# Wider weight conversion, three-instruction operand sums, and the order of the first norms in a fused attention and Fourier-mixing kernel

## The chip, the cores and the metric

The kernel runs on one core of a Trainium2 chip. A core has a matrix engine (TensorE, "PE" in the profile, with its weight loads "PEld"), a vector engine (VectorE, "DVE"), a scalar engine (ScalarE, "ACT"), GpSimd ("POOL") and SyncE ("SP", which here only issues DMAs). Each engine works through its own queue in order and waits for the others by semaphores. The metric is the device time in microseconds, as the median of several runs.

## The reference

Attention over 4 batches, 8 heads, 768 tokens and 64 columns per head, then a Fourier mixing block over the 512 columns of all heads, all in float32:

```python
k_sum = k.reshape(B, H, nb, 32, D).max(axis=3)      # 24 blocks of 32 keys
v_sum = v.reshape(B, H, nb, 32, D).mean(axis=3)
scores_l = where(|i - j| < 16, q @ k.T / sqrt(D), -1e9)
scores_s = q @ k_sum.T / sqrt(D) + log(32)
a = softmax(concat(scores_l, scores_s));  attn = a @ concat(v, v_sum)
x = attn as (B, S, 512)
u = x + real(fft(fft(x, axis=1), axis=2))
un = (u - mean(u)) / sqrt(var(u) + 1e-6)
out = u + relu(un @ w_ch1) @ w_ch2                  # 512 -> 2048 -> 512
```

The two weight matrices arrive as 64-bit floats and are handled as pairs of 32-bit words.

## The kernel before, in words

**Stages.** Batch 0's attention runs first and by itself (`first_attention`, L844), for 4 pairs of heads: `prepare` turns q and k with products against an identity (L714) and takes the maxima of key blocks (L696); `wide_scores` makes band scores (L744) and summary scores (L748) in two halves, their exponentials (L750) and a mask product; `sum_values` puts the value sums into `vw` (L763); `wide_values` makes the weighted values (L771), divides by the sums and writes them to `x`. The folds that prepare `x` for the transform follow (`fold_sequence`, `fold_halves`, `fold_ends`). In this function the order on TensorE and VectorE is the program's, by `manual_schedule`; elsewhere a scheduler orders instructions by priority and readiness, except where `issue_after(mark)` puts an instruction behind a marked one.

Then comes `gen_fourier` (L1198) for batch 0: a transform over tokens (products `y`, L1232 and L1236, copied out by ScalarE at L1237 and L1238), and one over columns (products `mx`, L1259 and L1261, six tiles of 128 tokens). Each tile is added to `x`, its statistics are taken (L1266, L1267), and per half of three tiles a chain of 14 small VectorE instructions (L1279 to L1291) makes the norm's scale and shift by an inverse square root. Then every tile is normalised into `un` (L1304 on ScalarE for odd tiles, L1307 on VectorE for even ones), transposed (`unt`, L1312) and copied into `u` (L1313).

The dense part follows: `gen_hidden` (L1319) and `gen_out` (L1375), with both products by a Strassen-Winograd scheme: an operand's four blocks are joined by four sums or differences, and seven block products replace eight. `_left_sums` and `_right_sums` (L477, L484) make these sums. Operands are tiles with seven slots, in the order

```python
A11, A12, S3, A22, S1, S2_, S4 = range(7)
B11, T3, B21, B22, T1, T2, T4 = range(7)
A21, B12 = S3, T3
```

Batches 1 to 3 are the same, with a narrower form of attention (`gen_attention`, L974: scores L787 and L804, values L822 and L827) woven between the dense products of the batch before. `drive(...)` (L1478) steps several generators in turn, in given proportions and priorities.

**Weights.** While batch 0 runs, `gen_weights` converts the 64-bit weights: `load_raw` (L1057) fetches pieces of 512 columns into `words`, four buffers deep; `convert` (L1071) masks exponent and mantissa on VectorE (L1081, L1082), rescales both on ScalarE (L1083, L1084), puts in sign and low word on VectorE (L1086, L1088) and multiplies. Two such pieces and the sums make one weight tile (`make`, L1094), and 16 weights are made: 8 of `w_ch1` and 8 of `w_ch2`, in the order of `plan` (L1051). The finished tile is also stored for the later batches.

**Small tables.** At the start ScalarE's queue issues DMAs for `ident`, `wide`, `count`, `sel` and `half_of`. The last has 128 x 2 numbers and serves `vs`, the value sums of batch 1 and later: a memset and L1507 fill it. Loads of q, k, v, tables and raw weights go through SP's queue, in program order (`fetch`, L551).

Of the kernel before, what the change touches and what calls it, by code (L numbers as in the profile page):

```python
# [10 lines left out]
I32 = mybir.dt.int32  # L11
U32 = mybir.dt.uint32
AF = mybir.ActivationFunctionType
# [463 lines left out]
def _left_sums(tt, a):  # L477
    tt(a(S1), a(A21), a(A22), ALU.add)
    tt(a(S3), a(A11), a(A21), ALU.subtract)
    tt(a(S2_), a(S1), a(A11), ALU.subtract)  # L480
    tt(a(S4), a(A12), a(S2_), ALU.subtract)


def _right_sums(tt, b):  # L484
    tt(b(T1), b(B12), b(B11), ALU.subtract)
    tt(b(T2), b(B22), b(T1), ALU.subtract)
    tt(b(T3), b(B22), b(B12), ALU.subtract)
    tt(b(T4), b(B21), b(T2), ALU.subtract)


def _main_program(ctx, tc, q, k, v, moe_w_ch1, moe_w_ch2, out):
# [72 lines left out]
    dense_bank = bank  # L564

# [278 lines left out]
    def first_attention():  # L844
# [8 lines left out]
        for g in range(NP - 1):  # L853
            p[g + 1] = wide_scores(0, g + 1, (lambda: add_blocks(1)) if g == 1 else None)
            wide_values(0, g, p[g], x)
            if g == NP - 2:
                block_sums(1, 0)
            load_values(*following(0, g, 2))
            for par in range(2):
                fold_sequence(par, g)  # L860
            if g < NP - 2:
                prepare(0, g + 2)
                sum_values(0, g + 1)
            if g == NP - 3:
                load(1, 0)
                get_tables(0, lambda: load_raw(1))
                load_raw(2)
                sum_values(0, g + 2)
        fold_halves(0, 0)
        wide_values(0, NP - 1, p[NP - 1], x)  # L870
        for par in range(2):
# [102 lines left out]
    def gen_attention(b):  # L974
# [13 lines left out]
        for g in range(NP + 1):  # L988
# [22 lines left out]
            if g < NP:  # L1011
                held = scores(b, g)
                if (b, g) == (1, 1):
                    key_maxima(g)
# [12 lines left out]
            if (b, g) == (1, 0):  # L1027
                for h in range(2):
                    with tc.issue_after(marks["norm"]):
# [41 lines left out]
    def convert(piece, dst):  # L1071


        n = 2 * HD
        i = pieces.index(piece)
        load_raw(i + 3)
        raw = raws[i]
        tmp = words[:, 4096 + 1024 * (i % 2):5120 + 1024 * (i % 2)].rearrange("p (a n) -> p a n", a=2)
        low, high = raw.bitcast(U32)[:, :, 0], raw[:, :, 1]
        ex, man = tmp[:, 0, :].bitcast(I32), tmp[:, 1, :].bitcast(I32)  # L1080
        nc.vector.tensor_scalar(out=ex, in0=high, scalar1=0x7FF00000, scalar2=None, op0=ALU.bitwise_and)  # L1081
        nc.vector.tensor_scalar(out=man, in0=high, scalar1=0x000FFFFF, scalar2=None, op0=ALU.bitwise_and)  # L1082
        nc.scalar.activation(out=ex, in_=ex, func=AF.Relu, bias=rebias, scale=8.0)  # L1083
        nc.scalar.activation(out=tmp[:, 1, :], in_=man, func=AF.Copy, bias=1.0, scale=2.0 ** -20)  # L1084
# [3 lines left out]
        nc.vector.scalar_tensor_tensor(out=tmp[:, 1, :], in0=low, scalar=2.0 ** -52, in1=tmp[:, 1, :],  # L1088
                                       op0=ALU.mult, op1=ALU.add)
        yield  # L1090
        tt(dst, tmp[:, 1, :], tmp[:, 0, :], ALU.mult)
        yield

    def make(f, j):  # L1094
# [8 lines left out]
        for hh in range(2):  # L1103
            yield from convert((f, j, hh), wv[:, 2 * hh:2 * hh + 2].rearrange("p a n -> p (a n)"))
        if f == 1:
            _left_sums(tt, lambda i: wv[:, i])
# [3 lines left out]
        else:  # L1110
            _right_sums(tt, lambda i: wv[:, i])
# [37 lines left out]
    def get_w2(b, j):  # L1149
# [4 lines left out]
        if b == 1 and j < NC:  # L1154
            marks["load"] = fetch(out=w[:, 0:4], in_=dw2[j][:, 0:4])
            _right_sums(lambda *a: to_sum.append((tt, a)), lambda i: w[:, i])
# [41 lines left out]
    def gen_fourier(b):  # L1198
# [44 lines left out]
        norms = []  # L1243
        for half in range(2):
# [5 lines left out]
            for i in range(HT):  # L1250
# [4 lines left out]
                else:  # L1255

                    ps = bank([P, 2, HD], f"mx_{b}_{t}")
                    for par in range(2):
                        nc.tensor.matmul(ps[:, par, :], yt[:, half, 2 * par, cols], fd[:, 3 * par, :],  # L1259
                                         start=True, stop=False)  # L1260
                        nc.tensor.matmul(ps[:, par, :], yt[:, half, 2 * par + 1, cols], fd[:, 3 * par + 1 + half, :],  # L1261
# [325 lines left out]
```

## Time and profile before

| | before |
|---|---|
| median of 3 runs | 803.74 us (803.03 to 804.97) |
| the profiled execution | 806.53 us, of which the span 804.7 us |
| PE busy | 779.7 us (97%) |
| PEld busy | 568.9 us (71%) |
| DVE busy | 496.4 us (62%) |
| ACT busy | 231.5 us (29%) |
| POOL busy | 47.3 us (6%) |
| mean granted TensorE clock | 0.986 |

The span goes from the first to the last instruction. The page divides it into 40 slices of 20.1 us and gives each engine's busy share in tenths. A row "PEclk" gives the clock that TensorE was granted, in tenths of full speed. The timeline lists instructions in order of time, merged where several alike follow each other; in brackets stands how long the engine sat idle before, and which event ended the wait. A line number can be that of a helper: L567 is the one through which most two-input VectorE operations go, and L553 the one that issues DMAs.

### The profile page before, as it was taken

Reading aid. Unit: us, or ns where it says so; the run is one execution under the profiler, and the core shown is the slowest. Engines: PE = TensorE matmul, PEld = TensorE weight load, DVE = VectorE, ACT = ScalarE, POOL = GpSimd, SP = SyncE. Lnnn points to the kernel's source line nnn. Section 1 sums busy time; section 2 is a strip of 40 time slices with the busy share of each in tenths; the row PEclk is TensorE's granted clock in tenths of the full one; section 3 lists DMA queues with packets and bytes.
Section 4 is the critical chain, followed back from the end, with each engine's and each line's share of the span. In section 5 each row is a group of like instructions: output and inputs, shape, how many; then the busy total and the mean of one; then the engine's idle time right before and its main releaser. Section 6 shows DMA issues by size and latency. Waiting matters only on the chain.

```text
span 804.7 us, 14470 instructions
## 1 busy us (share of the span) xinstructions
PE 779.7 (97%) x5914; PEld 568.9 (71%) x5914; DVE 496.4 (62%) x1119; ACT 231.5 (29%) x523; POOL 47.3 (6%) x85
## 2 busy tenths in 40 slices
PE   7978899999999999999999999999999999999996
PEld 5767755445579866688569866688669875786685
DVE  3789799696988737663577635563576623533441
ACT  3542756535636112200126112210126102001200
POOL 0000000000000011200120010300130000000000
PEclk8999799999999999999999999999999999999999
DMA  9798398698665358995354159620513153105001
GB/s 225 144 263 189 120 273 256 230 240 279 167 204 161 79 171 185 259 148 131 123 189 138 54 190 194 175 86 1 229 56 138 53 196 140 57 0 230 0 27 55
DMA packets 133355, 121.84 MB, mean 151 GB/s; under 512 B 94464, under 2 KB 114912, under 8 KB 133088
## 3 DMA queue, kind: packets, MB, share of 16 engines
q1 hardware_dynamic: 132016, 118.53, 53.2%
q0 software_dynamic: 576, 2.10, 0.7%
q8 instruction: 48, 0.79, 0.4%
q10 hardware_dynamic: 688, 0.20, 0.1%
q14 instruction: 27, 0.22, 0.1%
HBM read 97.22 MB, written 23.59 MB: 150 GB/s over the span
## 4 chain that ended last, share of the span: by engine, by line
PE 86%; DVE 9%; ACT 2%; DMA 1%; issue 1%; ACTq 0%; DVEq 0%
PE hx L1338 19%; PE ox L1407 18%; PE hz L1338 9%; PE oz L1407 9%; PE hy L1338 5%; PE o L1384 5%; PE oy L1407 5%; PE y L1232 3%; PE mx L1191 2%; PE sc L787 2%; PE av L822 2%; PE unt L1312 2%; DVE w L567 1%; PE av L827 1%; DMA half<-c_half 1%; DVE x L567 1%
## 5 line engine op out<-in xcount | busy, mean ns | idle before, releaser
L1338 PE MATMUL hx<-u,w 128*128 128x384 f32 x512 | 185.1, 490 | 1.7 <-ACT h L1349 1.1
L1338 PEld LDWEIGHTS hx<-u,w 128*128 128x128 f32 x512 | 95.3, 190 | 70.4 <-ACT p L793 4.4
L1338 PE MATMUL hz<-u,w 128*128 128x384 f32 x256 | 93.5, 486 | 0.0
L1407 PE MATMUL oz<-w,s 128*128 128x256 f32 x336 | 81.5, 380 | 0.0
L1407 PE MATMUL ox<-w,s 128*128 128x256 f32 x336 | 80.3, 380 | 0.0
L1407 PE MATMUL ox<-w,h 128*128 128x256 f32 x336 | 79.9, 381 | 0.0
L567 DVE TENSOR_TENSOR x<-ox,x 128x256 f32<-128x256 f32 x84 | 35.3, 423 | 67.5 <-PE ox L1407 67.3
L1338 PEld LDWEIGHTS hz<-u,w 128*128 128x128 f32 x256 | 48.5, 190 | 34.3 <-ACT h L1357 0.9
L1407 PEld LDWEIGHTS ox<-w,h 128*128 128x128 f32 x336 | 63.0, 190 | 11.1 <-issue 1.2
L1407 PEld LDWEIGHTS ox<-w,s 128*128 128x128 f32 x336 | 63.0, 190 | 9.4 <-DVE x L567 0.8
L1407 PEld LDWEIGHTS oz<-w,s 128*128 128x128 f32 x336 | 63.4, 190 | 8.6
L1349 ACT COPY h<-hx 128x384 f32<-128x384 f32 x32 | 15.3, 477 | 185.0 <-PE hx L1338 185.0
L567 DVE TENSOR_TENSOR h<-hy,h 128x384 f32<-128x384 f32 x32 | 17.8, 557 | 48.8 <-PE hy L1338 48.6
L1338 PE MATMUL hy<-u,w 128*128 128x384 f32 x128 | 46.6, 487 | 0.6 <-DVE h L567 0.6
L567 DVE TENSOR_TENSOR h<-hx,h 128x384 f32<-128x384 f32 x32 | 17.8, 556 | 43.9 <-PE hx L1338 43.2
L1384 PE MATMUL o<-w,h 128*128 128x512 f32 x96 | 42.4, 596 | 0.4 <-DVE w L567 0.4
L1368 ACT ACTIVATE h<-hx 128x384 f32<-128x384 f32 x32 | 15.7, 491 | 87.6 <-PE hx L1338 87.4
L1407 PE MATMUL oy<-w,h 128*128 128x256 f32 x168 | 40.1, 380 | 0.0
L1338 PEld LDWEIGHTS hy<-u,w 128*128 128x128 f32 x128 | 24.2, 190 | 17.4 <-DVE h L567 0.7
L567 DVE TENSOR_TENSOR x<-oz,x 128x256 f32<-128x256 f32 x42 | 17.8, 423 | 29.0 <-PE oz L1407 28.7
L1407 PEld LDWEIGHTS oy<-w,h 128*128 128x128 f32 x168 | 31.8, 190 | 4.4
L1384 PEld LDWEIGHTS o<-w,h 128*128 128x128 f32 x96 | 17.9, 190 | 22.9 <-issue 20.5
(164 smaller groups left out, 1098.8 us busy)
## 6 DMA issues: line engine op xcount, KB each, us to landing
w<-dw SPq DMA_DIRECT2D x44, 896.0 KB, 5.8
words<-in_moe_w_ch_dram SPq DMA_DIRECT2D x32, 512.0 KB, 6.1
dw<-w SPq DMA_DIRECT2D x12, 896.0 KB, 7.3
vw<-in_v_dram SPq DMA_DIRECT2D x47, 192.0 KB, 5.4
out_dram<-x SPq DMA_DIRECT2D x23, 256.0 KB, 2.0
vb<-in_v_dram SPq DMA_DIRECT2D x24, 192.0 KB, 6.5
kn<-in_k_dram SPq DMA_DIRECT2D x9, 384.0 KB, 6.0
qn<-in_q_dram SPq DMA_DIRECT2D x9, 384.0 KB, 6.8
```

The lines of the kernel that those rows point to most:

```text
L567: return nc.vector.tensor_tensor(out=out, in0=in0, in1=in1, op=op).ins
L787: nc.tensor.matmul(ps[h][r:r + 64, i, :], kt[rows, o:o + 64], qt[rows, o:o + BLOCK], start=True, stop=True)
L822: nc.tensor.matmul(av[r][32 * j:32 * (j + 1), t, :], p[rows, h, i - NB2 * h, :], vw[rows, i, :], start=(t == 0), stop=False, skip_group_ch ...
L827: ins = nc.tensor.matmul(av[r][:, t:t + HT + 1:HT, :], pm[rows, P * t:P * (t + 1)], vs[rows], start=False, stop=(t == HT - 1), skip_group_ ...
L1191: nc.tensor.matmul(out, y[:, g], table, start=False, stop=True, skip_group_check=True)
L1232: nc.tensor.matmul(y, fgs[b][par][:, st, P * g:P * (g + 1)], fs[par][:, g % 2, st, :], start=(st == 0), stop=(st == n - 1))
L1312: nc.tensor.transpose(ps[:, d // 2, d % 2, :], un[:, t, P * d:P * (d + 1)], ident)
L1338: ins = nc.tensor.matmul(ps, w[:, a, kk, :], u[:, r, kk, :], start=start and kk == 0, stop=stop and kk == 1, skip_group_check=True)
L1349: nc.scalar.copy(out=c11, in_=X)
L1368: nc.scalar.activation(out=c21, in_=X, func=AF.Relu)
L1384: nc.tensor.matmul(ps, h[:, n, hf, P * t:P * (t + 1)], wt[2, b, j][:, 2 * hf:2 * hf + 2, :], start=(n, hf) == (0, 0), stop=(n, hf) == (NC ...
L1407: nc.tensor.matmul(ps, left[a][:, n, :], wt[2, b, j][:, r, :], start=start and n == 0, stop=stop and n == NC - 1, skip_group_check=True)
```

## The change

There are five edits.

1. `convert` takes a whole weight of 1024 columns; its scratch for the mantissa is the destination itself. The masking of the exponent and its rescaling are in a helper `exponents`, which for all but the first two weights runs at the end of the weight before. `words` is used as two raw buffers of 1024 columns.
2. `_left_sums` and `_right_sums` use three instructions, of which one covers two slots by a strided view.
3. In batch 0, the d_model products of each tile are put behind those of the tile before; the first half is normalised as soon as its norm is there; additions of the last two tiles stand behind the first half's normalisation; the scores of batch 1's first pair stand behind the last d_model product, and some small operations get other marks.
4. In `first_attention` the values of pair 2 are made between the halves of pair 3's scores, folds of a pair stand behind the preparation of the next but one, and three products whose result is not used (`keep_busy`) stand behind the last values.
5. `half_of` is loaded through SP's queue behind `near`, and the filling of `vs` stands behind batch 0's last fold. The steps of `drive` are divided anew: the transform up to the last d_model tile with the first weights, then the rest with more weights and the attention of batch 1, whose preparation comes ahead of all this.

The diff, cut to its core:

```diff
-def _left_sums(tt, a):
-    tt(a(S1), a(A21), a(A22), ALU.add)
-    tt(a(S3), a(A11), a(A21), ALU.subtract)
-    tt(a(S2_), a(S1), a(A11), ALU.subtract)
-    tt(a(S4), a(A12), a(S2_), ALU.subtract)
...
+def _left_sums(tt, w):
+    tt(w[:, S1], w[:, A21], w[:, A22], ALU.add)
+    tt(w[:, S3:S2_ + 1:S2_ - S3], w[:, A11:S1 + 1:S1 - A11], w[:, A21::A11 - A21], ALU.subtract)
+    tt(w[:, S4], w[:, A12], w[:, S2_], ALU.subtract)
...
+    def keep_busy(n, src, cols=512):
+        ps = bank([P, cols], "busy")
+        for _ in range(n):
+            nc.tensor.matmul(ps, ident, src[:, 0:cols], start=True, stop=True)
...
+        def finish_pair(g):
             wide_values(0, g, p[g], x)
             if g == NP - 2:
                 block_sums(1, 0)
             load_values(*following(0, g, 2))
+        def finish_last_but_one():
+            finish_pair(NP - 2)
             for par in range(2):
-                fold_sequence(par, g)
+                fold_sequence(par, NP - 2)
+        for g in range(NP - 1):
+            p[g + 1] = wide_scores(0, g + 1, (None, lambda: add_blocks(1), finish_last_but_one)[g])
             if g < NP - 2:
+                finish_pair(g)
                 prepare(0, g + 2)
                 sum_values(0, g + 1)
+                for par in range(2):
+                    fold_sequence(par, g)
...
         wide_values(0, NP - 1, p[NP - 1], x)
+        keep_busy(3, p[NP - 1][:, 0].rearrange("p n c -> p (n c)"))
...
-                held = scores(b, g)
+                with tc.issue_after(marks["tile"]) if (b, g) == (1, 0) else ExitStack():
+                    held = scores(b, g)
                 if (b, g) == (1, 1):
-                    key_maxima(g)
+                    with tc.issue_after(marks["mx", 0]):
+                        key_maxima(g)
...
-                    with tc.issue_after(marks["norm"]):
+                    with tc.issue_after(marks["un", 0]):
                         tt(held[0][:, h], held[0][:, h], near[:, h], ALU.mult)
...
+    def exponents(m):
+        high = words[:, 2048 * (m % 2):2048 * (m % 2 + 1)].bitcast(I32).rearrange("p (n w) -> p n w", w=2)[:, :, 1]
+        ex = words[:, 4096 + 1024 * (m % 2):5120 + 1024 * (m % 2)].bitcast(I32)
+        nc.vector.tensor_scalar(out=ex, in0=high, scalar1=0x7FF00000, scalar2=None, op0=ALU.bitwise_and)
+        nc.scalar.activation(out=ex, in_=ex, func=AF.Relu, bias=rebias, scale=8.0)
...
+    def convert(m, dst):
+        load_raw(2 * m + 4)
...
+        if m < 2:
+            exponents(m)
         nc.vector.tensor_scalar(out=man, in0=high, scalar1=0x000FFFFF, scalar2=None, op0=ALU.bitwise_and)
+        nc.scalar.activation(out=dst, in_=man, func=AF.Copy, bias=1.0, scale=2.0 ** -20)
         yield
         nc.vector.scalar_tensor_tensor(out=ex, in0=high, scalar=-(1 << 31), in1=ex,
                                        op0=ALU.bitwise_and, op1=ALU.bitwise_or)
+        nc.vector.scalar_tensor_tensor(out=dst, in0=low, scalar=2.0 ** -52, in1=dst, op0=ALU.mult, op1=ALU.add)
         yield
+        tt(dst, dst, tmp, ALU.mult)
+        if 0 < m < NIT - 1:
+            exponents(m + 1)
         yield
...
+        def normalise(half, *which):
...
+                    marks["un", half] = nc.vector.tensor_scalar(...).ins
...
+                    with tc.issue_after(marks["tile"]) if t else ExitStack():
                         for par in range(2):
...
+                    marks["tile"] = ins.ins
...
+                    with tc.issue_after(marks["un", 0]) if t > HT else ExitStack():
+                        tt(xv, ps, xv, ADD)
...
+            if b == 0 and half == 0:
+                normalise(half)
...
-    nc.scalar.dma_start(out=half_of, in_=dr["half"].ap())
...
     fetch(out=near, in_=dr["near"].ap().rearrange("p (h i) c -> p h i c", h=2))
+    fetch(out=half_of, in_=dr["half"].ap())
...
-    nc.vector.memset(vs, 0.0)
-    nc.vector.tensor_scalar(out=vs[:, :, D], in0=half_of, scalar1=float(BLOCK), scalar2=None, op0=ALU.mult)
+    with tc.issue_after(marks["fold", 0]):
+        nc.vector.memset(vs, 0.0)
+        nc.vector.tensor_scalar(out=vs[:, :, D], in0=half_of, scalar1=float(BLOCK), scalar2=None, op0=ALU.mult)
...
-    drive((gen_fourier(0), 4, 600), (first(weights, 66), 12, 0), (first(attn, 6), 1, 0))
+    next(attn)
+    mixing = gen_fourier(0)
+    drive((first(mixing, 14), 14, 600), (first(weights, 27), 27, 0))
+    drive((mixing, 6, 600), (first(weights, 15), 15, 0), (first(attn, 5), 5, 0))
...
-            drive((most, 5, 0), (weights, 15, 0), (attn, 1, 0))
+            drive((most, 5, 0), (weights, 10, 0), (attn, 1, 0))
```

## The prediction

> **What bounds the kernel now.** I read the page's busy slices first. TensorE is at 9 tenths from slice 6 to the end, so the last 700 us are a stream of products in which a shorter VectorE or ScalarE instruction buys nothing by itself. Only the first five slices (100 us) have holes, and there the granted clock is under full speed too.
>
> ```profile
> PE   7978899999999999999999999999999999999996
> ...
> DVE  3789799696988737663577635563576623533441
> ...
> PEclk8999799999999999999999999999999999999999
> ```
>
> Next the timeline of TensorE and of VectorE in the first 60 us (start, length, instructions; in brackets the idle time before it and who ended it):
>
> ```profile
> 11.86 1.49 PE L748 MATMUL sc<-qt,km 64*32 64x384 f32 x4 [2.91 <-DVE km L696]
> 13.28 2.18 PE L744 MATMUL sc<-qt,kt 64*96 64x64 f32 x24
> ...
> 20.62 1.24 PE L744 MATMUL sc<-qt,kt 64*96 64x64 f32 x24
> ```
>
> ```profile
> 10.78 0.17 DVE L1507 TENSOR_SCALAR vs<-half 128x2 f32<-128x2 f32 x1 [8.61 <-DMA half<-c_half]
> ...
> 44.41 1.03 DVE L567 TENSOR_TENSOR p<-p,wide 128x384 f32<-128x384 f32 x2 [1.16 <-ACT p L750]
> ```
>
> VectorE stands 8.61 us for a 1 KB table that nothing needs until batch 1, and the key maxima (L696) queue behind it. TensorE therefore idles 2.91 us and then runs at half clock: the same 24 score products take 2.18 us here and 1.24 us later. Last, the stage between the d_model transform (L1259/1261, over at 74.64) and the first hidden products:
>
> ```profile
> 80.21 2.79 PE L1312 MATMUL unt<-ident,big 128*128 128x128 f32 x12 [3.20 <-DVE norm L1288]
> ...
> 99.02 0.86 PE L1338 MATMUL hx<-u,w 128*128 128x384 f32 x2
> ```
>
> ```profile
> 78.90 0.15 DVE L1291 TENSOR_TENSOR norm<-stat,norm 128x3 f32<-128x3 f32 x1
> ...
> 82.80 0.16 DVE L1291 TENSOR_TENSOR norm<-stat,norm 128x3 f32<-128x3 f32 x1
> ```
>
> The first half's norm is finished only at 78.90, because its 14 small instructions alternate with the second half's additions and statistics. Two windows of that stage and the next one tell who is short there (PE, PEld, DVE, ACT, POOL, clock, DMA, GB/s):
>
> ```profile
> 74.64:99.00 24.36, 18.46 (x367) 15.40 (x367) 18.45 (x58) 15.53 (x31) 0.00 (x0) 0.79 0.38 108
> 99.00:143.15 44.15, 43.41 (x339) 25.75 (x339) 42.39 (x89) 29.28 (x58) 0.00 (x0) 1.00 0.94 256
> ```
>
> In the second, TensorE (43.4 of 44.15) and VectorE (42.4) are both full: weights are converted just in time. So an earlier start is worth something only if both get it.
>
> **The change, part by part.** I sum it as the moment at which the stream begins, since the stream itself (99 to 804) hardly changes.
>
> *(1) The table `half` and the `vs` fills leave the start.* L1507 waits behind `fold` now. The key maxima run when kt is copied (6.99), so from 7.05 to 8.0; the first summary scores follow the band scores at 8.95 instead of 11.86: 2.9 us. With no hole the clock stays up: four groups are now slow (1.49 for 0.84 twice, 2.18 for 1.24, 2.23 for 1.53), 2.9 us, of which some is lost waiting for loads. I checked the loads by issue plus landing: qn of pair 1 lands at 13.1 (wanted at 13.0), vw of pair 0 at 14.7 to 16 (wanted 19.9), kn/qn of pair 2 at 18.6/20.7 (wanted 21.4), vw of pair 1 by 26 (wanted 28.3). SP issues without a pause from 5.2 to 24.9, so these times stand; they are just met. Walking the chain gives av of pair 0 at 19.95, now 25.12: **-5.2**. Ends: 0 if loads hold it back, 5.8 at most. The `half` DMA goes to SP behind `near`; one issue of some 0.4 us there, wanted by nobody before 70 us.
>
> *(2) `wide_values` of pair 2 between the halves of pair 3's scores.* It adds no instruction. VectorE is the bound there: from 32.24 to 58.09 it has little idle time but the 1.16 us at 44.41, and its reciprocals and products for pair 2 now fill that. **-1.2** (ends 0, -1.2). The folds moved behind `prepare` keep their total.
>
> *(3) Idle products.* Three of 512 columns, two instructions each, 0.43 us apiece by the output stage (40 of them in 17.36 us): 2.6 us on TensorE at about 42 to 44.5. They lie in a stretch where TensorE waits for VectorE's folds (47.5 to 52.4 has 1.3 us of work), so they cost nothing; without that cover they would cost 2.6. They push the q/k transposes of batch 1 to about 46, just when the token transform may start. What they buy: the transform runs at half clock from 52.4 to 55.8, losing 1.6 us. Here the Trainium skill, "TensorE: Matmul & The Clock Gate", section "Why this matters for your kernels", asks for no idle gap above about 3 us, since one idle window drops the clock. In this trace the longest gap there is 2.1 us and the clock fell all the same. By the rule the products buy 0, by the row 1.6. I take the row: **-1.6**.
>
> So the token transform starts at about 46.2 and the last d_model tile is done near 66.5 instead of 74.64: -8 (5.2 + 1.2 + 1.6).
>
> *(4) d_model tiles in order, first norm at once.* The three first tiles now finish together at 69.37, since their products are interleaved; in order they finish 3.5 and 1.7 us earlier, so additions and statistics (0.60 each) start under the transform. The first norm (14 instructions, some 2 us when nothing is between them) is ready before the last tile, and the transposes follow at once: the 5.57 us from 74.64 to 80.21 shrink to nothing. What is then late is ScalarE: exp, six half copies of norms and u, eight q/k copies, the value sums, 8.6 us or so in its queue before the av products that the second transposes wait for. These waits remain. The added waits: scores of (1,0) stand behind the last d_model tile, which is where they ran anyway; the additions of tiles 4 and 5 stand behind the first norm (1 to 2 us, behind them statistics and the second norm, which is still ready at about 70 and not 82.80); the key maxima of (1,1) behind the second norm, wanted only by L804 near 80. The half clock in this stage costs some 4 us more today (transposes 2.79 and 2.56 for 1.5; L822/827 4.2 for 2.2). From 24.4 us to 14.5 if the clock holds.
>
> Against this speaks the same page, Part 4 "PE-mode transpose": transposes do not count as activity for the gate. The row for it:
>
> ```profile
> 83.10:86.50 3.40, 1.78 (x14) 1.40 (x12) 1.67 (x5) 3.35 (x7) 0.00 (x0) 0.99 0.40 118
> ```
>
> 1.78 us of work, nearly all transposes, and the next 6.8 us came at half clock. It cannot tell the rule from mere idleness, but the new stage still holds some 6 us of transposes. By the row's fuller pipe 14.5 us, by the rule one more half-clock window, 16.2. I take 16: **-8.4**, ends -4 and -10.
>
> *(5) Conversion at 1024 columns.* Of one weight today, from the pitch between neighbours: two tensor_scalars at 0.34 and three two-input operations at 0.60, twice: 4.96 us. The line behind it, of the costliest groups of the first 235 us:
>
> ```profile
> L1086 DVE SCALAR_TENSOR_TENSOR words<-words 128x512 int32<-128x512 int32 x32 | 22.0, 687 | 4.1 <-ACT words L1083 3.8
> ```
>
> Half of each pitch grows with columns and 0.07 does not: 2 x 0.61 + 3 x 1.13 = 4.6. So 0.35 saved, plus 0.07 for the sums in three instructions. Sums of 12 weights and 16 conversions: some 6 us of VectorE, and about 8 of ScalarE (721 and 623 ns for 512 columns). Beside a full TensorE this is worth nothing by itself; it decides whether the weights keep up. VectorE from 74.64 to the last weight of the first output (148.8) does 65.6 us of work and idles 8.5. Off go about 2 (norm already done) and 2.6 (seven weights): 61. Started at 66.5, with half of the idle time or all of it kept, it is ready at 132 or 136: **-16.6 to -12.7**. TensorE by (1) to (4) is at -16.4. The smaller, with VectorE in the middle, is about -15.
>
> Sum: 804.7 - 15 = 790 for the span; the profiled execution took 806.53, and the median of the runs shown, 803.74, is 2.8 below it. So 803.74 - 15 = **789 us**.
>
> **Rivals.**
> A. *Loads hold the start.* DMA is at 0.8 to 1.4 share until 30 us and two wanted times were met by under 1 us. Then (1) gives 0 to 2 and the rest stays: 793.5. Against: landings do not depend on compute there.
> B. *Weights pace the stream.* VectorE is 96% busy in 99 to 143; if its queue, with coarser instructions of 1.2 us between small ones that TensorE waits for, gains only 7 to 9, the stream stalls in the hidden products: 796.
> C. *Slower: raw words arrive late.* Two buffers of 1024 columns in place of four of 512 make the request for the next weight wait for a whole conversion, and `exponents` of the next weight sits in VectorE's queue at the end of the present one. Landings take 6.2 us median (up to 11.7), a conversion 4.6 plus what is woven in. A stall over 1.1 us at each of 13 later weights eats the 15 us; at 1.5 us the time is 808. For: DMA share 0.94 in that stage. Against: VectorE's other work makes the pace 7 to 9 us a weight.
> D. *Early gains are absorbed by the attention of batch 1*, so that nothing arrives at the stream: 803.
>
> **Chances.** Forecast 0.62 (784 to 792.5), A 0.14, B 0.16, C 0.05, D 0.03. 0.2% (1.6 us) is about what a measurement of this kernel can tell from no change. Faster 0.92, same 0.03, slower 0.05. The range 783 to 798 takes in A and B and, at the low end, part (4) at -10 with the last 2 us of TensorE's idle time after 99.
>
> **What would show it.** L696 first at about 7, no 2.9 us before L748, full clock in 10 to 20 us; av of pair 0 near 20; full clock in the token transform and its start near 46; the first L1291 before the last L1261, the second some 4 us after; the first hidden products near 81 to 86; PE idle under 2 us after that. Wrong if hidden products start early but TensorE then waits for `w`, if VectorE waits on DMAs of `words`, or if av of pair 0 stays at 25.

## The result, and the profile after

The changed kernel takes **794.7 us** (median of 4 runs, 793.70 to 795.14) against 803.38 us (802.56 to 804.97) for the kernel before (4 runs, among them the three of the table above): ratio 0.989, interval 0.987 to 0.991. The forecast was 789 us, 783 to 798. The sign and the range were right; 8.7 us were gained where 14.7 were promised.

The profiled execution took 793.70 us, its span 791.9. First its busy slices:

```profile
PE   8998999999999999999999999999999999999997
...
DVE  5899988787988556752758544653677623533352
...
PEclk9999999999999999999999999999999999999999
```

The clock has no 7 or 8 left in its first five digits, VectorE's first slice has gone from 3 to 5, and TensorE's first five slices have filled up. Line numbers have shifted: the key maxima are L700, the wide scores L748 and L752, the small-operation helper L571, the norms L1313 to L1325, the transposes L1342, the hidden products L1368. The start, TensorE and then VectorE:

```profile
8.10 1.24 PE L748 MATMUL sc<-qt,kt 64*96 64x64 f32 x24
9.26 0.84 PE L752 MATMUL sc<-qt,km 64*32 64x384 f32 x4
10.03 1.24 PE L748 MATMUL sc<-qt,kt 64*96 64x64 f32 x24
```

```profile
7.42 0.95 DVE L700 TENSOR_REDUCE km<-kt 128x24 f32<-128x768 f32 x1 [5.39 <-ACT kt L719]
```

The key maxima wait for their own input (kt) and no more for a table; the summary scores follow the band scores without a hole, and both groups of band scores take 1.24 us. Next the stage between the two transforms, where the small operations of the norm and the transposes meet:

```profile
68.26 0.15 DVE L1322 SCALAR_TENSOR_TENSOR norm<-norm 128x3 f32<-128x3 f32 x1
...
70.03 0.16 DVE L1325 TENSOR_TENSOR norm<-stat,norm 128x3 f32<-128x3 f32 x1
```

```profile
70.97 1.62 PE L1342 MATMUL unt<-ident,big 128*128 128x128 f32 x12 [0.49 <-DVE big L1273]
...
78.65 0.94 PE L831 MATMUL av<-vs,p 64*128 64x130 f32 x12 [0.63 <-ACT vs L816]
79.53 1.53 PE L1342 MATMUL unt<-ident,big 128*128 128x128 f32 x12
```

The first half's norm is there at 70.03 instead of 78.90 and the transposes start after a wait of 0.49 us instead of 3.20; the two groups of twelve take 1.62 and 1.53 us instead of 2.79 and 2.56. Between the groups no wait of TensorE is longer than 0.64 us.

**The account by stage.** I cut both traces at the same events and took windows between them (columns: window, length, busy time of PE, PEld, DVE, ACT and POOL with instructions, granted clock, DMA share, GB/s). The stage from the last d_model product to the first hidden product that needs the sums of u (hz), before and then after:

```profile
74.71:101.01 26.30, 20.40 (x373) 16.55 (x373) 20.39 (x61) 17.48 (x35) 0.00 (x0) 0.81 0.35 100
```

```profile
0.00:20.20 20.20, 18.10 (x216) 12.01 (x216) 10.37 (x26) 7.68 (x15) 1.86 (x8) 1.00 0.93 213
...
46.62:68.19 21.57, 21.26 (x115) 18.82 (x116) 20.37 (x43) 10.06 (x28) 0.00 (x0) 1.00 1.09 246
68.19:90.06 21.87, 19.10 (x382) 13.43 (x382) 20.96 (x54) 18.06 (x35) 0.00 (x0) 1.00 0.83 190
90.06:131.77 41.71, 40.54 (x327) 23.96 (x326) 36.02 (x56) 24.58 (x44) 0.00 (x0) 1.00 0.74 221
```

Length minus PE's busy time is TensorE's idle time. All such windows together (us):

| stage | before: length (idle) | after: length (idle) | change | forecast |
|---|---|---|---|---|
| start to first value product of pair 0 | 25.12 (4.59) | 20.20 (2.10) | -4.92 | -5.2 |
| to the token transform | 27.64 (4.60) | 26.42 (1.23) | -1.22 | -1.2 |
| to the last d_model product | 21.95 (0) | 21.57 (0.31) | -0.38 | -1.6 |
| to the first hz | 26.30 (5.90) | 21.87 (2.77) | -4.43 | |
| to the first output product | 42.14 (0.74) | 41.71 (1.17) | -0.43 | -8.4 (with the row above) |
| to batch 0's last output stage (ox) | 88.82 (1.64) | 89.02 (1.95) | +0.20 | 0 |
| to the end | 572.73 (7.47) | 571.11 (6.04) | -1.62 | 0 |
| span | 804.70 | 791.90 | -12.80 | -14.7 |

Between these two executions the forecast failed by 1.9 us only, and that is in part luck: up to the first output product, parts (1) to (4) were to give 16.4 us and gave 11.4 (the first five rows; 1.4 of the 16.4 had been taken off for the weights), while 1.4 us came behind it, where the forecast had 0. The cause of those 1.4 us was not looked for. The other 4 us of the miss lie between an execution and a median: the profiled execution of before stands 3.1 us above the median of its runs, that of after 1.0 below.

### The profile page after: what moved, and what is told of

Its sections match the earlier page's. It is cut to its first block, busy times and chain, and to the rows that moved or that the text cites. A ratio compares the mean times of both kernels' runs of the same rounds, so it can differ in the third digit from the quotient of the medians.

```text
span 791.9 us, 14352 instructions
## 1 busy us (share of the span) xinstructions
PE 776.3 (98%) x5920; PEld 562.9 (71%) x5920; DVE 492.0 (62%) x1019; ACT 224.7 (28%) x491; POOL 47.9 (6%) x85
## 4 chain that ended last, share of the span: by engine, by line
PE 88%; DVE 5%; ACT 4%; DMA 2%; issue 1%; DVEq 0%
PE hx L1368 19%; PE ox L1437 18%; PE hz L1368 9%; PE oz L1437 9%; PE hy L1368 5%; PE o L1414 5%; PE oy L1437 5%; PE y L1252 3%; PE sc L791 2%; PE mx L1211 2%; PE av L826 2%; PE unt L1342 1%; PE av L831 1%; DMA qn<-in_q_dram 1%; PE ss L808 1%; ACT kt L727 1%
## 5 line engine op out<-in xcount | busy, mean ns | idle before, releaser
L1368 PE MATMUL hx<-u,w 128*128 128x384 f32 x512 | 185.4, 491 | 2.4 <-ACT h L1385 1.0
L1368 PEld LDWEIGHTS hx<-u,w 128*128 128x128 f32 x512 | 95.2, 190 | 71.3 <-ACT p L797 3.8
L1368 PE MATMUL hz<-u,w 128*128 128x384 f32 x256 | 93.0, 486 | 0.0
L571 DVE TENSOR_TENSOR x<-ox,x 128x256 f32<-128x256 f32 x84 | 35.5, 422 | 66.2 <-PE ox L1437 65.9
L1368 PEld LDWEIGHTS hz<-u,w 128*128 128x128 f32 x256 | 48.6, 190 | 33.9
L571 DVE TENSOR_TENSOR h<-hy,h 128x384 f32<-128x384 f32 x32 | 17.8, 557 | 48.9 <-PE hy L1368 48.8
L1368 PE MATMUL hy<-u,w 128*128 128x384 f32 x128 | 46.8, 487 | 0.0
L571 DVE TENSOR_TENSOR h<-hx,h 128x384 f32<-128x384 f32 x32 | 17.8, 556 | 45.2 <-PE hx L1368 44.0
L571 DVE TENSOR_TENSOR x<-oz,x 128x256 f32<-128x256 f32 x42 | 17.8, 423 | 30.4 <-PE oz L1437 30.1
L1368 PEld LDWEIGHTS hy<-u,w 128*128 128x128 f32 x128 | 24.2, 190 | 17.1 <-DVE h L571 0.7
```

Source lines behind the costliest of these rows:

```text
L571: return nc.vector.tensor_tensor(out=out, in0=in0, in1=in1, op=op).ins
L1368: ins = nc.tensor.matmul(ps, w[:, a, kk, :], u[:, r, kk, :], start=start and kk == 0, stop=stop and kk == 1, skip_group_check=True)
```

## The experiments

Ten edited kernels and the two unedited ones ran, in three groups; each is compared with runs of the kernel before on its own chip. "Stage" below is the time from the last d_model product to the first output product (68.44 us before, 63.58 after).

### The start alone

```diff
 kernel before
-    nc.scalar.dma_start(out=half_of, in_=dr["half"].ap())
 ...
     fetch(out=near, ...)
+    fetch(out=half_of, in_=dr["half"].ap())
 ...
+    with tc.issue_after(marks["fold", 0]):
         nc.vector.memset(vs, 0.0)
         nc.vector.tensor_scalar(out=vs[:, :, D], ...)
```

> The kernel before with one edit: `half_of` is loaded behind `near` and the filling of `vs` stands behind the last fold. Theory 1 (what starts earlier ends earlier): the start gains 5 us and passes it on to the end, less the part that was half clock only in the profiled execution: 798.5 to 800, from 803.4. Theory 2 (the weights pace the stream): an earlier start is eaten in 90 to 150 us: 802 to 803.

Measured: 801.67 us (22 runs) against 803.89 (53 runs), ratio 0.9966 (0.9953 to 0.9979): 2.2 to 2.7 us. In its profile the first value product of pair 0 starts at 20.64 and the clock is full until 48. The 4.5 us won by then against the profiled before are 2.2 to 2.7 us in the median, which lies between the two theories: part of it belongs to that one execution alone (next run).

### The kernel before, profiled a second time

No edit.

> The kernel before, profiled once more. Theory A (the profiled execution stood for the others): L1507 waits some 8.6 us for `half`, the summary scores some 2.9 us behind the band scores, half clock in 10 to 20 us. Theory B (that execution was an unlucky one): `half` lands 6 to 7 us after its issue as in the two kernels above that load it first, the summary scores wait 0.5 to 0.7 us, the clock at the start is full, and the first weighted values start near 20.8, not 25.1.

Measured: 804.87 us, span 803.0 (804.7 in the first profile). TensorE and VectorE at the start:

```profile
11.86 0.84 PE L748 MATMUL sc<-qt,km 64*32 64x384 f32 x4 [1.87 <-DVE km L696]
```

```profile
10.79 0.17 DVE L1507 TENSOR_SCALAR vs<-half 128x2 f32<-128x2 f32 x1 [8.62 <-DMA half<-c_half]
```

The table lands as late as in the first profile, but TensorE waits 1.87 us instead of 2.91, the same four summary scores take 0.84 instead of 1.49, and the slice of low clock is 3.4 us long instead of 6.8. The first value product of pair 0 comes at 23.75, not 25.12. So 1.37 of the 1.7 us between the two executions arise exactly in the stall that the change removes. Of the expectations theory A holds, with a shorter stall; the clock is not full, as B wanted.

### The change without its start

```diff
 changed kernel
+    nc.scalar.dma_start(out=half_of, in_=dr["half"].ap())
-    fetch(out=half_of, in_=dr["half"].ap())
 ...
-    with tc.issue_after(marks["fold", 0]):
+    (both instructions ahead of first_attention, as before)
```

> The changed kernel with the load of `half_of` and the filling of `vs` as before. Theory 1: 798.5 to 800, from 794.7, with the 8.6 us wait of VectorE for `half` back in the trace. Theory 2: 795 to 796.

Measured: 799.53 us (16 runs, 796.5 to 806.2), ratio 0.9952 (0.9932 to 0.9973); some 5 us worse than the change, as theory 1 said. But not at the start:

```profile
10.12 0.83 PE L752 MATMUL sc<-qt,km 64*32 64x384 f32 x4 [0.55 <-DVE km L700]
```

```profile
9.04 0.17 DVE L1537 TENSOR_SCALAR vs<-half 128x2 f32<-128x2 f32 x1 [6.87 <-DMA half<-c_half]
```

Here the same table, requested at the same place, is used at 9.04, 1.75 us sooner than in both profiles of before. TensorE waits 0.55 us, its clock stays full, and pair 0's values start at 20.61, 0.4 us later than in the change. The profiled 5 us are in the stage, which is 68.60 us long instead of 63.58. Two things make it so. First, the clock is at half speed from 77.7 to 84.6 (second transposes 2.82 us instead of 1.53, the value product ahead of them 1.67 instead of 0.94, score products 2.15 instead of 1.60): some 2.8 us. Second, TensorE idles 5.97 us instead of 3.94. Its list agrees with the change's for the first 1102 products, up to the first hidden ones, and differs from there on, though no edit was made in that stage: the list is made by a scheduler that weighs readiness times, and a load and two small instructions at the start were enough to have it choose another order. The low clock begins ahead of the place where the lists part, so the new order accounts for a part of the 5 us at most. The kernel also spreads more: its four runs at a mean clock of 0.999 or 1.000 take 796.5 to 797.5 us, the rest, at 0.991 to 0.997, reach 806.

### The conversion alone

```diff
 kernel before
-    four sums, conversion in pieces of 512 columns
+    three sums, conversion in pieces of 1024 columns
-    drive((gen_fourier(0), 4, 600), (first(weights, 66), 12, 0), ...)
+    drive((gen_fourier(0), 4, 600), (first(weights, 42), 8, 0), ...)
```

> The kernel before with the 1024-column conversion and the three-instruction sums alone (steps of the generators scaled to the same pace). Theory 1: TensorE is full behind it, so 802.5 to 804. Theory 2: 797 to 799, since VectorE (96% busy in 99 to 143 us) is what the stream follows.

Measured: 804.5 us (22 runs), ratio 1.0014 (0.9996 to 1.0032): nothing, as part (5) and theory 1 said. The stage is 68.97 us long. This kernel loads the table as the kernel before does, and yet its stall is short:

```profile
9.36 0.17 DVE L1510 TENSOR_SCALAR vs<-half 128x2 f32<-128x2 f32 x1 [7.19 <-DMA half<-c_half]
```

TensorE waits 0.62 us for the key maxima, and pair 0's values start at 20.93. So of four profiles with the old start two have the long stall (25.12 and 23.75 us) and two have not (20.93 and 20.61).

### The change with the old conversion

```diff
 changed kernel
-    three sums, conversion in pieces of 1024 columns
+    four sums, conversion in pieces of 512 columns
-    (first(weights, 27), 27, 0) ... (first(weights, 15), 15, 0) ... (weights, 10, 0)
+    (first(weights, 43), 43, 0) ... (first(weights, 24), 24, 0) ... (weights, 15, 0)
```

> The changed kernel with the 512-column conversion and the four-instruction sums of before (steps scaled back). Theory 1: 795 to 797, the loss being only VectorE's 2.6 us more work up to the first output product. Theory 2: 800 or more.

Measured: 798.32 us (6 runs), ratio 0.9932 (0.9907 to 0.9957), 3.5 us worse than the change and between the two expectations; the stage is 70.28 us long in its profile, which is the slowest of the six runs (801.14). ScalarE's conversion pieces come to lie between the two scalings of the summary values (L816), the value product behind them waits 1.47 us, and the clock is low from 77.9 to 91.6.

### The change with the old norms

```diff
 changed kernel
-                    with tc.issue_after(marks["tile"]) if t else ExitStack():
+                    with ExitStack():
 ...
-                    with tc.issue_after(marks["un", 0]) if t > HT else ExitStack():
+                    with ExitStack():
 ...
-            if b == 0 and half == 0:
-                normalise(half)
 (scores, key maxima and mask products at their old marks)
```

> The changed kernel with the first norms as before: no order among the d_model tiles, normalising only in the loop of the transposes, the old marks. Theory of the forecast (this is the largest part, 8.4 us): 801 to 803, first hidden products near 95. Rival (ScalarE's queue, the q/k copies ahead of the value sums, sets the second transposes anyway): 796 to 798.

Measured: 799.95 us (6 runs), ratio 0.9945 (0.9925 to 0.9965), 4.5 us worse than the change, between the two expectations; stage 69.52 us, the first hidden products at 94.78, as the theory said. The old wait is back, shorter than it was:

```profile
75.47 1.66 PE L1338 MATMUL unt<-ident,big 128*128 128x128 f32 x12 [2.53 <-DVE norm L1320]
```

TensorE's idle time in the stage is 9.55 us, against 3.94 in the change; the clock is at half speed from 76.7 to 86.9, too.

### The change with the old order of pairs, and without idle products

```diff
 changed kernel, old pairs
-    finish_pair(2) between the halves of pair 3's scores; folds behind prepare
+    values and folds of each pair behind the next pair's scores, as before
```

> The changed kernel with the values of pair 2 behind both halves of pair 3's scores and the folds in their old places. Forecast step: 1.2 us back in the folds, 795.9. Rival (the order of everything behind it decides more than this): off by 2 or more either way.

```diff
 changed kernel, no idle products
-        keep_busy(3, p[NP - 1][:, 0].rearrange("p n c -> p (n c)"))
```

> The changed kernel without the three idle products. Forecast step: the token transform runs half clocked for 3.4 us and 1.6 us are lost: 796.3, from 794.7. Rival (the transform then waits for the folds less, so the clock costs little): 795 with the half clock in the record.

Measured: 796.56 us (ratio 0.9908, 0.9887 to 0.9928) and 796.45 us (0.9898, 0.9877 to 0.9918), 6 runs each (795.9 and 796.3 were forecast); in the ratio 1.5 and 0.7 us worse than the change. Both intervals overlap with the change's (0.987 to 0.991), so the medians alone do not settle either; the profiles must. Without the new pairs, the stretch from pair 0's values to the token transform takes 27.45 us instead of 26.42; the stages behind it are alike to 0.2 us. Without the idle products:

```profile
50.82 2.38 PE L1251 MATMUL y<-fs,fold 128*128 128x193 f32 x8 [1.56 <-ACT fold L934]
52.99 2.03 PE L1255 MATMUL y<-fs,fold 128*128 128x193 f32 x6
```

A wait of 1.56 us stands ahead of the transform, the clock is at half speed from 51.4 to 54.8, and the first eight products take 2.38 us where they take 1.48 in the change; the stretch to the last d_model product is 23.04 us instead of 21.57. (This profile is the slowest of its six runs, 800.19 us. Its start is that of the change, but TensorE waits 2.41 us for the load of qn, the clock falls behind that wait, and pair 0's values start only at 24.68: the loads can hold the new start back.)

### The second weight behind the sums of u

From the second transposes to the first hz the change takes 10.53 us (79.53 to 90.06), the kernel before 9.78, although the transposes have become faster. VectorE's timeline of the change in that stretch:

```profile
82.82 1.22 DVE L1108 SCALAR_TENSOR_TENSOR w<-words,w 128x1024 f32<-128x1024 uint32 x1
83.95 1.75 DVE L571 TENSOR_TENSOR u<-u 128x1536 f32<-128x1536 f32 x1
85.62 1.22 DVE L571 TENSOR_TENSOR w<-w,words 128x1024 f32<-128x1024 f32 x1
86.75 0.95 DVE L571 TENSOR_TENSOR u<-u 128x768 f32<-128x768 f32 x1
```

Conversion instructions of 1.2 us (w) stand between the sums of u that the first hz needs. My second theory was that these cost the missing 3.7 us.

```diff
 changed kernel
                 yield
+                if (f, j) == (1, 1):
+                    stage = ("us", 0)
+                    while stage not in issued:
+                        yield
 ...
-        _right_sums(tt, u.rearrange(...))
+        (the same, with the last sum marked ("us", b))
 ...
+    drive((first(weights, 12), 12, 0))
```

> The changed kernel, with one step: of the second w1 weight only the two maskings and ScalarE's two passes stay where they are; its two scalar_tensor_tensor instructions, its product and its sums wait for batch 0's last u sum (L1346). Theory (the term of the sum that fell short is the second half of the norms' stage: from the second transposes at 79.5 us to the first hidden product that needs the u sums at 90.1 us, 10.5 us, because VectorE puts conversion instructions of 1.2 us between the u copies and the u sums, about 3.7 us in all): that stretch falls to 7.5 to 8.8 us, the first output product moves by the same 2 to 3 us, and the time is 791.5 to 793.5 us. Rival (the sums wait for ScalarE's copies and TensorE's own queue, and the conversion lies in their shadow): the stretch stays at 10 us or more and the time at 794 to 795.5 us. Second rival (the second weight is now late): the stretch falls, but TensorE waits 1 to 3 us for the second weight's sums before the second group of hidden products, and the time is 794 to 797 us.

Measured: 794.79 us (6 runs, 794.04 to 796.42) against 795.66 for the change in the same group. The instructions did change places:

```profile
83.46 1.75 DVE L571 TENSOR_TENSOR u<-u 128x1536 f32<-128x1536 f32 x1
...
86.93 0.95 DVE L571 TENSOR_TENSOR u<-u 128x768 f32<-128x768 f32 x1
...
89.13 1.21 DVE L1106 SCALAR_TENSOR_TENSOR words<-words 128x1024 int32<-128x1024 int32 x1
```

From the second transposes to the first hz it is now 9.06 us, not 10.53, but the stage is 63.56 us long, as before this edit (63.58). The two profiles do not have the same clock, however. This one has a slice at half speed from 78.2 to 81.6, which the first profile of the change has not:

```profile
78.52 1.67 PE L831 MATMUL av<-vs,p 64*128 64x130 f32 x12 [0.62 <-ACT vs L816]
80.12 2.23 PE L1346 MATMUL unt<-ident,big 128*128 128x128 f32 x12
```

These take 0.94 and 1.53 us in the change, so 1.4 us of this stage are clock. The second profile of the change (below) has such a slice too, and a stage of 65.12 us. Of the 1.6 us between it and this one, 0.8 go to a group of summary scores that stands whole here and is cut in two there (see part (4) at the end), and 0.2 to the slow slice, which costs 1.6 us there. About 0.6 us is left for the edit, where 2 to 3 were expected; the median, 0.9 us lower, is within the spread of the runs. So the theory has fallen in size. The first rival has the time right (794 to 795.5 us), though not its stretch of 10 us or more. The first hz was a bad landmark: in the change TensorE idles only 0.6 us between 79.5 and 99, so what moved ahead of the first hz was mostly work that it had to do anyway.

### The scaling ahead of the copies, both steps together, and the change again

```diff
 changed kernel
+            if (b, g) == (1, 0):
+                scale_sums(b, g)
             if n1:
                 prepare(*n1, ...)
-            if b == 1:
+            if b == 1 and g:
                 scale_sums(b, g)
```

> The changed kernel, with ScalarE's two scalings of the summary values of batch 1's first pair (L816) ahead of the eight copies of its second pair's keys and queries (L727) instead of behind them. Theory (the second transposes, which are held behind that pair's value product L831, start at 79.5 us because the scaling stands behind 4.2 us of copies on ScalarE): the scaling runs near 74 us, and the second transposes begin up to 2 us earlier; but the second norm is ready only at 77.56 us and its first scaled tile takes ScalarE 0.81 us more, so they begin near 78.4 us, 1.1 us earlier, and the time is 793 to 794.5 us. Rival (TensorE's fill between the halves was work that it has to do anyway, and is done later at the same cost): second transposes earlier, first output product unmoved, 794.5 to 795.5 us.

> The changed kernel with both steps: the second weight's last instructions behind batch 0's u sums, and the scaling of the summary values ahead of the eight copies. Theory: the two add up, since one shortens the stretch before the second transposes and the other the one behind them: first hidden product that needs the u sums at 86.5 to 88.5 us instead of 90.1, time 790.5 to 792.5 us. Rival (the order in which the program's scheduler puts small instructions decides, and a new order costs as much as it brings): 793.5 to 796 us.

> The changed kernel once more, unaltered, on the same chip as the three others: 794.2 to 795.2 us, ratio 0.987 to 0.990. Its second profile shows how far the landmarks move from execution to execution: under the theory that the table of halves sets the start no more, the first value product of pair 0 at 20 to 20.7 us, with TensorE's clock at full speed throughout; if the loads set it, one at 21 us or more and a slice at a lower clock.

Measured, 6 runs each on one chip (before: 804.5 us, 11 runs):

| kernel | median, us | range | mean clock | ratio to before | stage in its profile |
|---|---|---|---|---|---|
| change again | 795.66 | 794.48 to 796.91 | 0.9962 | 0.9887 (0.9860 to 0.9913) | 65.12 |
| second weight later | 794.79 | 794.04 to 796.42 | 0.9977 | 0.9883 (0.9856 to 0.9910) | 63.56 |
| scaling first | 793.36 | 790.43 to 795.35 | 0.9992 | 0.9859 (0.9829 to 0.9888) | 62.68 |
| both | 792.99 | 791.68 to 795.79 | 0.9993 | 0.9859 (0.9829 to 0.9888) | 62.04 |

The scaling now runs at 74.08 us, ahead of the copies, and the value product that needs it no longer waits. The second transposes are still no earlier:

```profile
79.53 1.53 PE L1344 MATMUL unt<-ident,big 128*128 128x128 f32 x12 [0.90 <-ACT big L1272]
```

They wait for a scaled tile that ScalarE starts at 78.66 us, when the eight copies are through. So the expectation's instant was wrong by 1.1 us, and that the time fell into its range is luck. What did shorten the stage in the profile, by 0.9 us against the first of the change, is mainly another thing: the third group of summary scores isn't cut in two here.

```profile
103.48 0.85 PE L808 MATMUL ss<-qt,km 64*32 64x384 f32 x8 [0.57 <-ACT p L797]
```

That saves 0.8 us. The rest of the 2.3 us in the median may be clock: 0.003 more of 794 us are 2.4 us at most. The second profile of the change shows what is avoided: its clock is at half speed from 79.3 to 82.7 and from 209.0 to 212.4 us, and its stage is 1.5 us longer than in the first. Why the edited order keeps the clock up oftener was not tried. The change again took 0.5 us more than the range given for it, and its pair 0's values start at 20.74, between the two marks set, with the clock full until 79.3. "Both" missed its range by 0.5 us, though its first hz came as told, at 87.76; against "scaling first", both at full clock in the stage, its stage is 0.64 us shorter, about what the later second weight gave above. "Both" has the lowest median of all kernels and is faster than the kernel before; the intervals of the last three ratios overlap with the change's, so its lead over the change, 0.3%, is likely and not settled.

## Why the prediction was right, and where not

**What bounds the kernel** was read rightly: 11.4 of the 12.8 us gained between the profiled executions lie in the first 132 us. There TensorE's idle time fell by 8.3 us (15.83 to 7.58 over the first five rows of the table), and from there to the end by 1.1.

**(1) The start: right to 0.3 us** between the profiled executions (-5.2, -4.92; pair 0's values at 20.20 instead of the 19.95 worked out). The loads met their times but for 0.41 us of waiting for qn of pair 1, named there as met by under 1 us. Rival A is out for both profiles of the change (20.20 and 20.74), though not for every execution: in the kernel without idle products the loads held the same start back to 24.68. The measured median, 794.7 us, is as near to the times of rivals A (793.5) and B (796) as to the forecast; the number alone doesn't tell them apart, the landmarks do.

**(2) The pairs: right** (-1.2; 1.0 in the kernel with the old order), and by the mechanism given: VectorE's idle time between pair 0's values and the token transform fell from 4.53 to 3.38 us, with the same work (23.11 and 23.04 us).

**(3) The idle products: the mechanism right, the sum short.** They raise the clock as the row said: the transform's first eight products take 1.48 us, not 2.94 (before, then after),

```profile
52.76 2.94 PE L1232 MATMUL y<-fs,fold 128*128 128x193 f32 x8
```

```profile
46.62 1.48 PE L1252 MATMUL y<-fs,fold 128*128 128x193 f32 x8
```

and taking the idle products out costs 1.47 us up to the last d_model product (-1.6 was counted). The longest wait shortly ahead of the transform is 2.10 us in the profile of before and 1.56 in the kernel without idle products, and the clock falls in both (at the start of before it fell behind waits of 2.91 and 1.87 us). All are under the 3 us that the Trainium skill ("TensorE: Matmul & The Clock Gate", section "Why this matters for your kernels") gives as the limit of an idle gap; the row decides. But the stretch itself shrank by 0.38 us: a few of its products between 50.9 and 53.9 start 0.20 to 0.33 us apart instead of 0.16, which makes 0.5 us and whose cause wasn't looked for, one transpose of batch 1 has slipped in (0.27), and 0.31 us are spent waiting for ScalarE, whose two conversion passes of 1024 columns (1.20 and 1.10 us at 54.26) stand ahead of copies of y. That last wait is a price of part (5) that I hadn't counted.

**(4) The norms' stage: the mis-sized term.** It was to give 8.4 us: all of the 5.9 us of idle time, and 2.5 us of clock. Measured over the whole stage: 4.86. The parts are these.

- Idle time fell from 6.64 to 3.94, that is by 2.7 and not by 5.9. The forecast let it vanish and then spoke of waits on ScalarE that "remain" without putting them into the sum. They are what is left: 0.63 for L816, 0.9 around the value product, 0.45 for the copies of q, 0.49 for the first scaled tile, 1.2 in the stream behind.
- The clock gave 3.9 and not 2.5: transposes 5.3 to 3.1 us, value products 2.5 to 1.7, their summary part 1.7 to 0.9. The 1.5 us that I had set aside for one more slow slice, by the same page's rule on transposes (Part 4, "PE-mode transpose"), weren't due in the profiled execution, though they were in the second profile of the change; whether the transposes or the waits near them brought that slice, no run tells apart.
- 1.7 us came back from a cost that I hadn't thought of. Eight summary-score instructions in a row take 0.85 us, before:

```profile
76.16 0.85 PE L804 MATMUL ss<-qt,km 64*32 64x384 f32 x8
...
127.42 0.85 PE L804 MATMUL ss<-qt,km 64*32 64x384 f32 x8
```

after, two of the three groups are cut in two:

```profile
69.65 0.83 PE L808 MATMUL ss<-qt,km 64*32 64x384 f32 x2
...
72.52 0.84 PE L808 MATMUL ss<-qt,km 64*32 64x384 f32 x6
...
103.52 0.83 PE L808 MATMUL ss<-qt,km 64*32 64x384 f32 x2 [0.57 <-ACT p L797]
...
116.18 0.84 PE L808 MATMUL ss<-qt,km 64*32 64x384 f32 x6
```

Two take as long as eight, and six as long as eight. The eight work on four different places of the array (64 rows by 32 columns each), two on one place, and I read the times so that different places run beside each other only while they are neighbours in TensorE's list. Transposes or hidden products in between make it 1.67 us instead of 0.85. The kernel with the scaling first bears this out: its third group stands whole and takes 0.85 us. A sum by instructions and mean duration cannot see this: the mean is 495 ns in both pages.

Together: -2.7 - 3.9 + 1.7 = -4.9, which closes the account. The first norm was ready not before the last tile but 1.8 us behind it, at 70.03: its 14 instructions took 3.8 us and not 2, with sums of the first weight (66.08 to 68.3) and a tile's statistics between them, the same weaving that I had blamed in the kernel before. Over the second norm I was off in the same way (77.56, foretold about 70).

**(5) The conversion** is worth nothing by itself, as said (ratio 1.0014). In the changed kernel, taking it back costs 3.5 us. But that isn't shown to be a price of VectorE time: in its profile ScalarE's order and 13.7 us at half clock lengthen the stage, and the start edit alone, taken back, also made the stage 5 us longer, by another order and a low clock. The single worth of conversion and norms inside the change is therefore not settled by these runs; only that the norms need their edit (2.53 us of old wait without it). The length of the wide instructions was estimated well: they follow each other at 0.61 us (mask) and 1.13 us (two inputs), as worked out. But the pace of the weights was over-estimated. The last weight that TensorE waits for in the first output, before and then after:

```profile
148.83 6.28 PE L1384 MATMUL o<-w,h 128*128 128x512 f32 x14 [0.37 <-DVE w L567]
```

```profile
137.81 7.13 PE L1414 MATMUL o<-w,h 128*128 128x512 f32 x16 [0.72 <-DVE w L571]
```

It came 11.0 us earlier, not 12.7 to 16.6. TensorE's own path had moved by 11.4, so the weights cost 0.35 us more of waiting, and not the 1.4 us that the forecast took off for them. Of the rivals, C is out: VectorE waits 0.7 us in all for raw words. B is half right: the stream does wait for a weight, but by 0.72 us; conversion passes do stand ahead of small copies, but moving those of the second weight away shortened the stage by about 0.6 us only. D is out.

**The step that cost most of the gap: 803.74 - 15.** I formed the gain on the profiled execution (806.53 us) and subtracted it from a median 2.8 us lower. About half of that surplus was a variable part of the very stall that the change removes (1.37 us are gone in the second profile), so it couldn't be had twice. Measured from median to median the start is worth 2.2 to 2.7 us, not 5.2. From 806.53 the sum would have given 791.5, 2.2 below the profiled 793.70. Within the sum, part (4) is the largest shortfall: 8.4 foretold, 4.9 measured.

**What was to show it** came as told for the key maxima (7.42), the hole before the summary scores (gone), the clock, pair 0's values (20.20), the token transform (46.62) and the first hidden products (82.52). It came otherwise for the norms, whose two instants (70.03 and 77.56) were given as ahead of the last d_model product, here 68.19, and some 4 us later.

## What to carry to other kernels

A stall with a low clock in it differs from execution to execution; profile the kernel twice before a gain is read from such a stall, and form the sum from that kind of number that it will be held against. Account for a stage in idle time and busy time separately: here three effects of 2.7, 3.9 and 1.7 us made one number of 4.9, and a landmark within a full stretch (the first hz) moved by 1.5 us while the stage gained much less. Compare stages of two profiles only at like clock: a low slice of 3.4 us made or hid differences of 1.4 to 1.6 us here. Where a scheduler lays out the instructions, an edit in one place can reorder another; compare the order of the lists and the clock before an ablation is read as the price of its edit.

## What the hardware showed unexpectedly

- The clock is an item of its own in the account. In these traces low slices last 3.41 us or a multiple of it (6.83, 10.24, 13.65), at half speed. Over the runs its mean was 0.9877 before (53 runs) and 0.9962 to 0.9975 after. As an estimate, (1 - clock) times the time is 9.9 us before and 2.0 to 3.0 after, so about 7 of the 9 us gained may be clock, an upper bound, since TensorE waits in part of those slices.
- One small load of 1 KB was used at 10.78 and 10.79 us in two profiles of before, and at 9.36 and 9.04 in two kernels that request it at the same place. What moved it was not tried.
- Two products on parts of the array take as long as eight (0.83 and 0.85 us); eight take 0.85 or 1.67, according to whether other products stand between them.
